# A chunked scan and two gated feed-forward layers on one core: a fourth raw-weight buffer and new queue orders

## The chip, the core and the metric

The kernel runs on one core of one Trainium2 chip. A core has five engines with a queue each: PE (TensorE, matrix products), DVE (VectorE), ACT (ScalarE), POOL (GpSimd) and SP (SyncE, which here issues every DMA). Each engine works through its queue strictly in order and waits on semaphores for the others. The metric is device time in microseconds; the kernel before takes 615.63 us (median of three runs, 614.98 to 616.26).

## The reference

Three stages follow each other. The first is a linear recurrence over 4 batches, 8 heads and 768 positions, done in chunks; the other two act on each of the 3072 tokens with 256 features and a hidden width of 2048.

```python
# stage 1, per batch and head (x: 768x32, B, C: 768x16, a: 768)
log_a = np.log(np.clip(a, 1e-06, 1.0))
M = einsum(C, B) * exp(cum_i - cum_j) * causal
y = M @ x + (C @ state) * exp(cum)
state = exp(sum(la)) * state + sum_j(B_j x_j * exp(cum_end - cum_j))
# stage 2: layer 1
h = x @ w_in;  x = (h * sigmoid(h)) @ w_out
# stage 3: layer 2
h = x @ w_in2
P = a[0] + a[1]*h + a[2]*h**2 + a[3]*h**3
Q = 1 + abs(b[0])*abs(h) + abs(b[1])*h**2
out = (P / (Q + 1e-06)) @ w_out2
```

## The kernel before

**Tiles.** The 3072 tokens are 24 tiles of 128. A tile's recurrence is one *visit* on PE (`visit`, L674): four products C B (tile `att`, 32x256), four with the carried state S, eight with the masked matrix M and the token values, four for the state update. Around it DVE multiplies by the mask (`M`, L657, twice a visit), splits the result into a high and a low float32r part (`y1l`, L762), and updates the state (`um`, L745, and `S`, L749). POOL builds the mask (`Gm`, L587, four instructions a visit) and scales B and C (L604, L626). ACT makes the high part (L759) and two parity copies of C (L615).

**Layers.** The hidden width is 16 slices f of 128. Per slice and per block of tokens PE does one group of six products into `h` (in-projection: high x high, high x low, low x high, two halves each) and one of six into `acc` (out-projection). Layer 1 runs over seven blocks of 2, 2, 4, 4, 4, 4 and 4 tiles, layer 2 over six blocks of four. Blocks 0 and 1 have 256 columns, the others 512. A slice of a block goes PE `h`, then ACT and the other vector engines, then PE `acc`; blocks follow each other strictly, slice 0 to 15.

**Weights.** The weights of a slice arrive as 64-bit floats in a raw buffer (`wraw`, 512 KB, a ring of three). ACT takes the exponent and top bits (L486), DVE shifts and joins the bits (L492, L494), ACT rounds to the high part (L510), and DVE or POOL subtracts for the low part (L514). Layer 1's 16 slices are kept in 16 fixed buffers `w`. Layer 2's 16 are prepared likewise in the raw buffer, stored to `w2s` in DRAM (L526) and read back (`w<-w2s`, L536) into the same 16 buffers as the last layer-1 block lets go of them.

**Layer 2's pointwise work.** Per slice ACT does the square (L896), the absolute value (L900), the logarithm of Q (L916) and its negative exponential (L919); POOL and DVE do the polynomial (L904, L907, L910, L913), DVE the product g (L925). Then g is rounded to its high part `gh` by ACT (L801) or by POOL (L803), and POOL subtracts for the low part `gl` (L807).

**What sets the order.** Nothing is ordered by hand. The code adds operations with the engines that may run them, a cost for each, their dependencies and a sort key. `Plan.run` (L124) is a list scheduler: it repeatedly takes, among what can start soonest, the operation of the smallest key, books its cost on the engine, and so fixes every queue's order, and for operations with a choice the engine. Keys come from the table `K` (L31) and costs from the `c_*` helpers and constants in the code; the plan's model holds the time an engine needs, a port that DVE and POOL share, a factor for DVE while a mask is built (`soft`), and a slower PE where PE has had few columns. On the chip the orders stay, the times are the chip's.

Of the kernel before, what the change touches and what calls it, by code (L numbers as in the profile page):

```python
# [24 lines left out]
WC = 2 * DM  # L25
# [3 lines left out]
HALVED = 0  # L29
TAIL_FLEX = 1  # L30
K = dict(  # L31
    t0=-4.418,
    step0=0.196,
    lag1=5.7,
    fo1=-117.341,
    fo2=113.649,
    fol=49.258,
    tab=-19.458,
    lead=-17.189,
    kt=5.507,  # L40
    kq=13.452,
    kl=16.822,
    kg=-1.533,
    ks=3.696,
    warm=23,
    warm0=5.147,
    warmstep=0.414,
    late=96.836,
    tab0=255.655,
    bulk=40.355,  # L50
    d0=-10.314,
    gap0=-1.906,
    d2=0.536,
    d3=-0.323,
    early2=28.205,
    early=88.368,
    w2a=-581.064,
    w2b=-104.957,
    w1=-58.843,
    w1step=-16.262,  # L60
    w1load=15.211,
    tokload=-28.356,
    ahead=-3.939,
    eps=0.032,
    step2=9.745,
    dT=[-7.22, -13.03, -30.38, -32.69, -14.27, -104.22, 51.53, 29.37, 26.09, 41.72, 4.01, -1.19],
    dD=[-119.66, -78.65, -1.57, 14.91, -69.27, 21.05, -99.93, -46.8],
    dW=[16.35, -10.16, -80.03, 81.03, -22.98, 4.59, 58.27, 59.37, 3.02, 47.31, 26.94, 7.79, -83.78, -4.56, -23.9, -13.94],
)
SET_LN_EXP, SET_SILU = 6, 18  # L70

# [37 lines left out]
class Plan:  # L109
# [9 lines left out]
    def add(self, choices, key, deps=(), new=(), use=(), wr=(), rd=(), cols=0, after=0.0, big=True, soft=False):  # L119
        op = Op(choices, key, list(deps), list(new), list(use), wr, rd, cols, after, big, soft)  # L120
        self.ops.append(op)
        return op

    def run(self):  # L124
        free = dict.fromkeys(("PE", "ACT", "DVE", "POOL", "SP"), 0.0)
        waiting = {}
        left = {}
        for op in self.ops:
            deps = set(op.deps)
            for b in op.new:  # L130
                i = b.ring.turns.index(b)
                if i:
                    deps.update(b.ring.turns[i - 1].users[:1])
                if i >= b.ring.n:
                    deps.update(b.ring.turns[i - b.ring.n].users)
            deps.discard(op)
            op.waits = deps
            left[op] = len(deps)
            for d in deps:
                waiting.setdefault(d, []).append(op)  # L140
        ready = [op for op in self.ops if not left[op]]
        for op in ready:
            op.ready = {e: op.after for e in op.choices}
        order = []

        port = [0.0]

        def shared(op, e):
            c = op.choices[e]
            return len(c) > 2 and c[2]  # L150


        wrote, was_read = {}, {}


        ticks = {}
        wide, soft = [True], [0.0]

        def length(op, e, start):
            t = op.choices[e][0]  # L160
            if e == "DVE" and shared(op, e) and start < soft[0]:
                t *= 1.3
            if op.soft:
                soft[0] = start + t
            if e == "PE":
                if op.big != wide[0]:
                    t += 0.1
                    wide[0] = op.big
                if ticks.get(int((start + self.TICK0) / self.TICK) - 1, 0) < 3060:
                    t *= 2  # L170
                for i in range(4):
                    k = int((start + self.TICK0 + (i + 0.5) / 4 * t) / self.TICK)
                    ticks[k] = ticks.get(k, 0) + op.cols / 4
            return t

        def when(op, e):
            t = max(free[e], op.ready[e])
            for b in op.wr:
                t = max(t, was_read.get(b, 0.0))
            for b in op.rd:  # L180
                t = max(t, wrote.get(b, 0.0))
            if shared(op, e):
                t = max(t, port[0])
            return t

        while ready:
            cand = [(when(op, e), op, e) for op in ready for e in op.choices]
            first = min(c[0] for c in cand) + K["eps"]
            est, op, e = min((c for c in cand if c[0] <= first), key=lambda c: (c[1].key, c[0], c[1].choices[c[2]][0]))
            ready.remove(op)  # L190
            op.start, op.eng = est, e
            op.end = est + length(op, e, est)
            free[e] = op.end
            if shared(op, e):
                port[0] = op.end
            for b in op.wr:
                wrote[b] = op.end + self.LAT[e]
            for b in op.rd:
                was_read[b] = max(was_read.get(b, 0.0), op.end + self.LAT[e])
            order.append(op)  # L200
            for o in waiting.get(op, ()):
                left[o] -= 1
                if not left[o]:
                    o.ready = {
                        q: max(d.end + (self.LAT[d.eng] if d.eng != q or q == "SP" else self.SELF[q]) for d in o.waits)
                        for q in o.choices
                    }
                    ready.append(o)
        assert len(order) == len(self.ops), "a cycle"
        return order  # L210
# [3 lines left out]
def ssd_moe_moe_kernel(ctx: ExitStack, tc: tile.TileContext, tok, la_in, consts, w1, w2, ab, outT):  # L214
# [11 lines left out]
    ACT, DVE, POOL, PE = nc.scalar, nc.vector, nc.gpsimd, nc.tensor  # L226
    plan = Plan()
    add = plan.add
# [3 lines left out]
    def ring(tag, n, cols, dt=F32, space="SB"):  # L232
        rings[tag] = (Ring(n), n, cols, space)
# [44 lines left out]
        PE.matmul(out, lhsT, rhs, start=start, stop=stop)  # L278

    def dma(key, nbytes, fn, deps=(), new=(), use=()):  # L280
        return add({"SP": (max(0.06, nbytes / 260e3), fn)}, key, deps, new, use)


    con = fixed("con", [P, C_CUM])
# [12 lines left out]
    wide = w1.dtype == U64  # L297
    for f in range(NF):
        ring(f"w{f}", 1, 2 * WC)
    ring("wraw", 3, 2 * WC)  # L300
    if wide:
        ring("wv", 6, WC)
    ring("tok", 4, TOK + DM)
# [36 lines left out]

    cum = new("cum")
    ld_la = dma(0.0, 98e3, lambda: (load_table(SET_LN_EXP), nc.sync.dma_start(la, la_in)))
    ld_c1 = dma(0.1, 70e3, lambda: nc.sync.dma_start(con[:, 0:C_MASK], consts[:, 0:C_MASK]))

    def f_cum():
# [291 lines left out]
    def cb_part(n):  # L637
        t, T, d, ld, o_bw, o_cx, o_cw, o_gm, Gm, x, bw, cw, bt, cx, e0, Ee = at[n]
        cb = R_cb.new(lambda: att)

        def f_cb():
            for q in range(4):
                r = slice(32 * q, 32 * q + 32)
                mm(att[q][:, 0:DM], bt()[r], cx()[r], True, True)

        return cb, f_cb
# [20 lines left out]
    def cb_alone(n):  # L667
        t, T, d, o_cx = at[n][0], at[n][1], at[n][2], at[n][5]
        cb, f_cb = cb_part(n)
        o_cb = add({"PE": (0.61, f_cb)}, T + 2 * d, [o_cx], new=[cb], use=[t], wr=range(4), cols=4 * DM, big=False)  # L670
        masked(n, cb, o_cb)


    def visit(n):  # L674

        t, T, d, ld, o_bw, o_cx, o_cw, o_gm, Gm, x, bw, cw, bt, cx, e0, Ee = at[n]
# [5 lines left out]
        pv = prev.get(n - 1) if c > 0 else None  # L682
# [13 lines left out]
        def f_u():  # L696
            for q in range(4):
                r = slice(32 * q, 32 * q + 32)
                mm(psu[r], bw()[:, r], x()[:, 64 * q : 64 * q + 64], True, True)

        us = c < TPB - 1
        if us:
            ub, sn = R_psu.new(lambda: psu), new("S")
        y_deps, y_use = o_m + [o_cw] + ([pv[1]] if pv else []), ms + [t] + ([pv[0]] if pv else [])
        y_len = 0.55 + (0.25 if pv else 0)
        if n < ALONE:
            o_y = add({"PE": (y_len, f_y)}, T + 5 * d, y_deps, new=[yb], use=y_use, wr=[0, 1], cols=P, big=False)
            if us:
                o_u = add({"PE": (0.21, f_u)}, T + 4 * d, [o_bw], new=[ub], use=[t], wr=[2], big=False)
            if n + 1 < min(NTB, ALONE + 1):  # L710
                cb_alone(n + 1)
        else:
            more = n + 1 < NTB
            if more:
                cb, f_cb = cb_part(n + 1)

            def f_visit():
                if more:
                    f_cb()
                f_y()  # L720
                if us:
                    f_u()

            o_y = o_u = add(
                {"PE": (y_len + (0.15 if us else 0) + (0.61 if more else 0), f_visit)}, T + 5 * d,
                y_deps + ([o_bw] if us else []) + ([at[n + 1][5]] if more else []),
                new=[yb] + ([ub] if us else []) + ([cb] if more else []), use=y_use + ([at[n + 1][0]] if more else []),
                wr=range(4), cols=P + (4 * DM if more else 0), big=False,
            )
            if more:  # L730
                masked(n + 1, cb, o_y)
# [249 lines left out]
    t = K["t0"]  # L981
# [68 lines left out]
    for op in plan.run():  # L1050
        fn = op.choices[op.eng][1]
# [69 lines left out]
```

## Time and profile before

| | |
|---|---|
| median of three runs | 615.63 us (614.98 to 616.26) |
| profiled execution | 617.0 us, its span 615.3 us |
| mean granted clock of PE | 0.986 |
| busy: PE, DVE, ACT, POOL | 601.0, 440.5, 399.1, 366.7 us |

The span is what the rows show; the profiled execution's own time is 1.7 us longer than its span. Busy shares are means over unlike stages: the early part, in which the weights of layer 1 are prepared and the first visits run, the six blocks of layer 1 after it, and layer 2 from about 320 us.

### The profile page before, as it was taken

Reading aid. Unit: us, or ns where it says so; the run is one execution under the profiler, and the core shown is the slowest. Engines: PE = TensorE matmul, PEld = TensorE weight load, DVE = VectorE, ACT = ScalarE, POOL = GpSimd, SP = SyncE. Lnnn points to the kernel's source line nnn. Section 1 sums busy time; section 2 is a strip of 40 time slices with the busy share of each in tenths; the row PEclk is TensorE's granted clock in tenths of the full one; section 3 lists DMA queues with packets and bytes.
Section 4 is the critical chain, followed back from the end, with each engine's and each line's share of the span. In section 5 each row is a group of like instructions: output and inputs, shape, how many; then the busy total and the mean of one; then the engine's idle time right before and its main releaser. Section 6 shows DMA issues by size and latency. Waiting matters only on the chain.

```text
span 615.3 us, 9815 instructions
## 1 busy us (share of the span) xinstructions
PE 601.0 (98%) x3442; PEld 478.4 (78%) x3445; DVE 440.5 (72%) x727; ACT 399.1 (65%) x751; POOL 366.7 (60%) x478
## 2 busy tenths in 40 slices
PE   8798999999999999999999999999999999999997
PEld 4476799877777778888888887878888878878875
DVE  4899897777543412322312899998998999999995
ACT  5675686656423311312335889998988998988984
POOL 5797783423332222212200789889888888888884
PEclk8798999999999999999999999999999999999999
DMA  6765567666200000000035800000000000000000
GB/s 222 257 184 180 163 243 242 226 231 236 91 27 2 0 1 1 0 1 0 1 102 178 267 2 0 1 35 1 1 35 1 36 2 0 35 2 0 35 2 35
DMA packets 18314, 47.30 MB, mean 77 GB/s; under 512 B 2136, under 2 KB 5336, under 8 KB 18264
## 3 DMA queue, kind: packets, MB, share of 16 engines
q1 hardware_dynamic: 18264, 46.67, 22.5%
q8 instruction: 27, 0.44, 0.3%
q14 instruction: 23, 0.19, 0.1%
HBM read 34.99 MB, written 11.67 MB: 76 GB/s over the span
## 4 chain that ended last, share of the span: by engine, by line
PE 87%; DVE 6%; POOL 2%; ACT 2%; issue 1%; DMA 1%; SPq 0%; DVEq 0%; ACTq 0%; POOLq 0%
PE acc L278 41%; PE h L278 34%; PE b L278 7%; PE att L278 5%; POOL Gm L587 1%; DVE wv L494 1%; POOL gl L807 1%; DMA tok<-in_tok_dram 1%; DVE M L657 1%; DVE gl L807 1%; DVE tok L913 1%; DVE g L925 1%; DVE h L910 0%; ACT wv L486 0%; ACT tok L615 0%
## 5 line engine op out<-in xcount | busy, mean ns | idle before, releaser
L278 PE MATMUL h<-y1h,w 128*128 128x512 f32 (+1 forms) x700 | 222.8, 376 | 1.1 <-POOL w L514 0.9
L278 PE MATMUL acc<-gh,w 128*128 128x512 f32 (+1 forms) x832 | 215.3, 380 | 1.0 <-ACT gh L801 1.0
L278 PEld LDWEIGHTS acc<-gh,w 128*128 128x128 f32 x832 | 149.8, 189 | 33.5 <-ACT gh L801 1.4
L807 DVE TENSOR_TENSOR gl<-T,gh 128x512 fp32r<-128x512 f32 (+1 forms) x101 | 68.0, 674 | 120.0 <-POOL gh L803 88.6
L278 PEld LDWEIGHTS h<-y1h,w 128*128 128x128 f32 x700 | 129.6, 190 | 29.5 <-DVE tok L913 2.1
L839 ACT ACTIVATE T<-h 128x512 f32<-128x512 f32 (+1 forms) x112 | 59.7, 534 | 118.5 <-PE h L278 111.4
L278 PE MATMUL h<-y1l,w 128*128 128x512 f32 (+1 forms) x350 | 130.4, 373 | 0.0
L807 POOL TENSOR_TENSOR gl<-g,gh 128x512 fp32r<-128x512 f32 x95 | 122.9, 1299 | 11.5 <-ACT gh L801 7.5
L803 POOL TENSOR_SCALAR gh<-T 128x512 fp32r<-128x512 f32 (+1 forms) x59 | 35.9, 608 | 154.7 <-ACT T L839 123.1
L278 PE MATMUL acc<-gl,w 128*128 128x512 f32 (+1 forms) x416 | 124.3, 379 | 0.2 <-DVE gl L807 0.2
L278 PEld LDWEIGHTS acc<-gl,w 128*128 128x128 f32 x416 | 76.3, 189 | 16.3 <-DVE gl L807 0.4
L904 POOL TENSOR_SCALAR tok<-T,abt 128x512 f32<-128x512 f32 x96 | 74.5, 776 | 11.6 <-ACT T L896 9.8
L278 PEld LDWEIGHTS h<-y1l,w 128*128 128x128 f32 x350 | 66.4, 190 | 11.4
L925 DVE SCALAR_TENSOR_TENSOR g<-tok,abt,b 128x512 f32<-128x512 f32 x96 | 71.3, 744 | 4.6 <-POOL gl L807 1.6
L907 DVE SCALAR_TENSOR_TENSOR b<-T,absb,b 128x512 f32<-128x512 f32 x96 | 71.8, 749 | 1.4 <-ACT b L900 1.4
L916 ACT ACTIVATE b<-b,lnb 128x512 f32<-128x512 f32 x96 | 63.6, 664 | 7.1 <-DVE b L907 6.3
L587 POOL TENSOR_SCALAR_AFFINE_SELECT Gm<-eG 128x256 f32<-128x256 f32 x96 | 55.4, 611 | 20.7 <-DVE M L657 14.0
L919 ACT ACTIVATE b<-b 128x512 f32<-128x512 f32 x96 | 56.3, 588 | 1.6
L910 DVE TENSOR_TENSOR h<-tok,h 128x512 f32<-128x512 f32 x63 | 43.4, 689 | 5.3 <-ACT b L900 5.3
L913 DVE SCALAR_TENSOR_TENSOR tok<-T,abt,h 128x512 f32<-128x512 f32 x63 | 46.7, 741 | 0.0
L278 PE MATMUL b<-y1h,w 128*128 128x512 f32 x132 | 46.4, 392 | 0.0
L803 POOL TENSOR_SCALAR gh<-g 128x512 fp32r<-128x512 f32 x59 | 36.8, 624 | 14.3 <-PE acc L278 12.5
(68 smaller groups left out, 649.6 us busy)
## 6 DMA issues: line engine op xcount, KB each, us to landing
wraw<-in_w_dram SPq DMA_DIRECT2D x32, 512.0 KB, 4.4
w2s<-wraw SPq DMA_DIRECT2D x16, 512.0 KB, 2.9
w<-w2s SPq DMA_DIRECT2D x16, 512.0 KB, 4.7
tok<-in_tok_dram SPq DMA_DIRECT2D x24, 320.0 KB, 3.0
out_dram<-Gm SPq DMA_DIRECT2D x12, 256.0 KB, 2.0
Ee<-dre SPq DMA_DIRECT2D x21, 66.5 KB
cum<-in_consts_dram SPq DMA_DIRECT2D x1, 320.0 KB
dre<-Ee SPq DMA_DIRECT2D x2, 66.5 KB
```

The costliest lines, as they stand in the source:

```text
L278: PE.matmul(out, lhsT, rhs, start=start, stop=stop)
L587: POOL.affine_select(g4[:, :, p * SUB : (p + 1) * SUB], eG[:, p, n * H : (n + 1) * H].unsqueeze(2).broadcast_to([P, H, SUB]), pattern=[[0, ...
L803: eng.tensor_scalar(gh.t[:, 0:W], g.t[:, 0:W], 1.0, 0.0, op0=ALU.mult, op1=ALU.add)
L807: eng.tensor_tensor(gl.t[:, 0:W], g.t[:, 0:W], gh.t[:, 0:W], op=ALU.subtract)
L839: ACT.activation(T.t[:, 0:W], h.t[:, 0:W], AF.Silu)
L904: POOL.tensor_scalar(t1.t[:, 0:W], s.t[:, 0:W], abt[:, 3:4], abt[:, 1:2], op0=ALU.mult, op1=ALU.add)
L907: DVE.scalar_tensor_tensor(c.t[:, 0:W], s.t[:, 0:W], absb[:, 1:2], c.t[:, 0:W], op0=ALU.mult, op1=ALU.add)
L910: DVE.tensor_tensor(h.t[:, 0:W], t1.t[:, 0:W], h.t[:, 0:W], op=ALU.mult)
L913: DVE.scalar_tensor_tensor(t1.t[:, 0:W], s.t[:, 0:W], abt[:, 2:3], h.t[:, 0:W], op0=ALU.mult, op1=ALU.add)
L916: ACT.activation(c.t[:, 0:W], c.t[:, 0:W], AF.Ln, bias=lnb)
L919: ACT.activation(c.t[:, 0:W], c.t[:, 0:W], AF.Exp, scale=-1.0)
L925: DVE.scalar_tensor_tensor(g.t[:, 0:W], t1.t[:, 0:W], abt[:, 0:1], c.t[:, 0:W], op0=ALU.add, op1=ALU.mult)
```

## The change

The ring of raw weights has four buffers instead of three. Four cost constants of the plan change: the rate of a DMA (260 to 380 KB per us), the length of a visit on PE, and the factor on DVE beside a mask (1.3 to 1.4). Nearly all numbers of the table `K` are new. No operation is added or removed; the numbers of PE, DVE and SP instructions are the same.

```diff
-    t0=-4.418,
+    t0=29.745,
...
-    w1load=15.211,
+    w1load=-66.668,
...
         def length(op, e, start):
             t = op.choices[e][0]
             if e == "DVE" and shared(op, e) and start < soft[0]:
-                t *= 1.3
+                t *= 1.4
...
     def dma(key, nbytes, fn, deps=(), new=(), use=()):
-        return add({"SP": (max(0.06, nbytes / 260e3), fn)}, key, deps, new, use)
+        return add({"SP": (max(0.06, nbytes / 380e3), fn)}, key, deps, new, use)
...
-    ring("wraw", 3, 2 * WC)
+    ring("wraw", 4, 2 * WC)
...
-        y_len = 0.55 + (0.25 if pv else 0)
+        y_len = 0.55 + (0.33 if pv else 0)
...
-                {"PE": (y_len + (0.15 if us else 0) + (0.61 if more else 0), f_visit)}, T + 5 * d,
+                {"PE": (y_len + (0.21 if us else 0) + (0.64 if more else 0), f_visit)}, T + 5 * d,
```

The orders that come out differ on every engine. The first place is DVE at the end of layer 1's weight preparation, in the kernel before. `w_67` is the buffer of slice 15, `wv` a weight under way, `gl` the low part of a layer-1 slice, `M`, `um`, `S` and `y1l` belong to visits.

```order
L657 TENSOR_TENSOR M_1063<-att_80,Gm_927 128x512
L762 TENSOR_TENSOR y1l<-att_80,y1h 128x2x128
L657 TENSOR_TENSOR M_1074<-att_81,Gm_927 128x512
L492 TENSOR_SCALAR wv_1078<-wv_1078 128x512
L749 SCALAR_TENSOR_TENSOR S_1096<-S_1007,Ee_772,um_1058 128x64
L494 SCALAR_TENSOR_TENSOR wv_1078<-wraw_998,wv_1078 128x512
L807 TENSOR_TENSOR gl_1123<-T_1115,gh_1117 128x256
L514 TENSOR_TENSOR w_67_1121<-wv_1078,w_67_1121 128x512
L762 TENSOR_TENSOR y1l<-att_80,y1h 128x2x128
```

And the same place in the changed kernel (the last row of both is the one behind slice 15's low part):

```order
L807 TENSOR_TENSOR gl_920<-T_855,gh_858 128x256
L494 SCALAR_TENSOR_TENSOR wv_884<-wraw_811,wv_884 128x512
L807 TENSOR_TENSOR gl_951<-T_897,gh_901 128x256
L492 TENSOR_SCALAR wv_947<-wv_947 128x512
L807 TENSOR_TENSOR gl_962<-T_942,gh_945 128x256
L494 SCALAR_TENSOR_TENSOR wv_947<-wraw_882,wv_947 128x512
L514 TENSOR_TENSOR w_64_953<-wv_884,w_64_953 128x512
L610 TENSOR_TENSOR tok_868<-tok_868,Ee_918 128x128
L514 TENSOR_TENSOR w_67_975<-wv_947,w_67_975 128x512
L745 TENSOR_TENSOR um_996<-att_81,con 128x64
```

Ahead of slice 15's low part DVE had the masks of twelve visits, and has those of nine: 18 instead of 24 multiplications `M`, 8 instead of 11 `y1l`, 5 instead of 8 each of `um` and `S`, 11 instead of 12 `gl`, but 10 instead of 9 low parts of weights and 9 instead of 8 scalings of C (L610). On PE twelve visits stood ahead of slice 15's first `h` group, and nine do now; the tenth now stands at the end of block 1, and the eleventh to the eighteenth between the groups of block 2, with two or three `h` or `acc` groups of 512 columns between two visits (eight of them, mostly, before). POOL builds 41 instead of 53 mask instructions in that stretch.

The second place is ACT in the middle of layer 2: `h` and `b` are banks of `h` or of the running Q, `T` the square. Before:

```order
L896 ACTIVATE T_4788<-h_3707 128x512
L916 ACTIVATE b_3494<-b_3494,lnb 128x512
L919 ACTIVATE b_3494<-b_3494 128x512
L900 ACTIVATE b_3492<-h_3707,abt 128x512
L916 ACTIVATE b_3493<-b_3493,lnb 128x512
L896 ACTIVATE T_4818<-b_3491 128x512
L919 ACTIVATE b_3493<-b_3493 128x512
L801 ACTIVATE gh_4831<-g_4793 128x512
L900 ACTIVATE b_3494<-b_3491,abt 128x512
```

After:

```order
L896 ACTIVATE T_4873<-h_3598 128x512
L900 ACTIVATE b_3471<-h_3598,abt 128x512
L801 ACTIVATE gh_4885<-g_4871 128x512
L919 ACTIVATE b_3472<-b_3472 128x512
L916 ACTIVATE b_3471<-b_3471,lnb 128x512
L896 ACTIVATE T_4901<-h_3670 128x512
L900 ACTIVATE b_3470<-h_3670,abt 128x512
L801 ACTIVATE gh_4913<-g_4899 128x512
L919 ACTIVATE b_3471<-b_3471 128x512
L916 ACTIVATE b_3470<-b_3470,lnb 128x512
```

Before, high parts `gh` stand on ACT for 37 of layer 2's 96 slice and block pairs and on POOL for 59; now for 80 and 16. One turn of ACT is now square, absolute value, `gh`, exponential, logarithm, in this order.

Of the other places two are told in words. Between the last layer-1 use of slice 0's buffer on PE and layer 2's first `h` group on it stood six groups of 512 columns (three `acc`, three `h`), and stand three (two `acc`, one `h`); the read of its layer-2 weights is issued behind that last use. And of layer 2, PE's order after the start is one `h` and one `acc` in turn, with `acc` six slices behind `h`, where it was eight.

## Rows read from the trace of the kernel before

**Rows 1.** Windows: stretch, length, busy (instructions) of PE, PEld, DVE, ACT, POOL; clock

```profile
0.00:8.59 8.59, 6.67 (x33) 3.69 (x34) 1.20 (x5) 3.91 (x10) 1.38 (x9) 1.00 0.74 225
8.59:27.90 19.31, 14.57 (x154) 8.86 (x155) 17.20 (x33) 12.41 (x29) 16.39 (x30) 0.73 0.69 237
27.90:54.00 26.10, 24.29 (x277) 18.52 (x278) 24.77 (x46) 19.81 (x51) 22.27 (x36) 1.00 0.64 205
54.00:66.00 12.00, 10.52 (x107) 8.16 (x108) 9.34 (x19) 4.96 (x13) 7.87 (x15) 0.72 0.44 142
66.00:76.70 10.70, 10.12 (x122) 7.97 (x120) 9.77 (x20) 7.30 (x19) 8.77 (x13) 1.00 0.54 176
76.70:108.30 31.60, 31.56 (x355) 28.81 (x356) 27.31 (x56) 22.28 (x56) 19.21 (x35) 1.00 0.71 242
400.00:600.00 200.00, 199.94 (x862) 160.58 (x861) 190.03 (x292) 180.70 (x318) 174.20 (x190) 1.00 0.04 14
```

**Rows 2.** Groups of DVE instructions, whole span, shapes apart

```profile
L657 DVE TENSOR_TENSOR M<-att,Gm 128x512 f32<-128x512 f32 x48 | 32.3, 682 | 1.4 <-ACT y1h L759 0.8 <-POOL tok L604 0.3
...
L807 DVE TENSOR_TENSOR gl<-T,gh 128x256 fp32r<-128x256 f32 x26 | 14.4, 556 | 2.2 <-ACT gh L801 1.1 <-issue 0.6 <-POOL gh L803 0.4
...
L762 DVE TENSOR_TENSOR y1l<-att,y1h 128x256 fp32r<-128x256 f32 x24 | 10.0, 416 | 6.3 <-ACT y1h L759 6.0 <-PE att L278 0.2
...
L610 DVE TENSOR_TENSOR tok<-tok,Ee 128x128 f32<-128x128 f32 x16 | 6.7, 421 | 1.5 <-DMA tok<-in_tok_dram 1.4
...
L749 DVE SCALAR_TENSOR_TENSOR S<-S,Ee,um 128x64 f32<-128x64 f32 x16 | 5.6, 353 | 0.1
...
L745 DVE TENSOR_TENSOR um<-att,con 128x64 f32<-128x64 f32 x16 | 3.5, 217 | 3.3 <-PE att L278 3.0 <-ACT Ee L419 0.3
```

**Rows 3.** Timeline of DVE from 65 to 77 us

```profile
66.02 0.69 DVE L494 SCALAR_TENSOR_TENSOR wv<-wraw,wv 128x512 uint32<-128x512 uint32 x1
...
69.97 0.91 DVE L494 SCALAR_TENSOR_TENSOR wv<-wraw,wv 128x512 uint32<-128x512 uint32 x1
...
75.98 0.70 DVE L514 TENSOR_TENSOR w<-wv,w 128x512 fp32r<-128x512 f32 x1
```

**Rows 4.** Timeline of POOL, the mask instructions beside it

```profile
68.70 2.49 POOL L587 TENSOR_SCALAR_AFFINE_SELECT Gm<-eG 128x256 f32<-128x256 f32 x4
```

**Rows 5.** Chain that ended last, 97 to 103 us: start, length, what

```profile
98.20 1.42 PE acc L278 x12
99.62 1.71 PE att L278 x40
101.33 0.92 PE acc L278 x6
```

**Rows 6.** Waits, 8.59 to 76.7 us: total, times, longest

```profile
PE att L278 <- DVE M L657: 4.4, 4, 2.5
...
DVE w L514 <- ACT w L510: 2.4, 3, 1.8
...
ACT wv L486 <- DMA wraw<-in_w_dram: 0.8, 2, 0.5
```

**Rows 7.** DMA issues of the page: KB each, median us to landing

```profile
w<-w2s SPq DMA_DIRECT2D x16, 512.0 KB, 4.7
```

**Rows 8.** All transfers that touch the tensor w2s

```profile
DMA to landing us min/median/max: 2.9/3.7/5.1
```

**Rows 9.** Timeline of ACT in layer 2

```profile
467.99 0.60 ACT L896 ACTIVATE T<-h 128x512 f32<-128x512 f32 x1 [0.66 <-PE h L278]
468.49 0.66 ACT L900 ACTIVATE b<-h,abt 128x512 f32<-128x512 f32 x1
469.06 0.63 ACT L801 ACTIVATE gh<-g 128x512 fp32r<-128x512 f32 x1
469.58 0.66 ACT L916 ACTIVATE b<-b,lnb 128x512 f32<-128x512 f32 x1
470.18 0.66 ACT L900 ACTIVATE b<-h,abt 128x512 f32<-128x512 f32 x1
```

More of the change, by code (lines that the diff above doesn't have):

```diff
@@ L31 @@
 K = dict(
-    t0=-4.418,
[L33 to L44, printed above, removed]
+    t0=29.745,
+    step0=29.431,
+    lag1=-8.285,
+    fo1=-11203.308,
+    fo2=3770.147,
+    fol=4732.874,
+    tab=348.639,
+    lead=521.411,
+    kt=-2007.807,
+    kq=185.136,
+    kl=885.523,
+    kg=-42.381,
+    ks=-46.369,
     warm=23,
@@ L47 @@
     warmstep=0.414,
[L48 to L60, printed above, removed]
-    w1load=15.211,
[L62 to L68, printed above, removed]
+    late=129.205,
+    tab0=262642.37,
+    bulk=-71.654,
+    d0=1.385,
+    gap0=-2.671,
+    d2=-175.049,
+    d3=1.526,
+    early2=13.234,
+    early=102.236,
+    w2a=-179.125,
+    w2b=922.116,
+    w1=27.105,
+    w1step=-47.852,
+    w1load=-66.668,
+    tokload=-25.637,
+    ahead=-12.045,
+    eps=0.045,
+    step2=553.546,
+    dT=[28.53, 94.46, -154.25, -63.99, -191.58, -193.3, 23.14, -88.64, 60.15, 62.96, 55.27, -29.82],
+    dD=[-161.27, -199.56, 54.31, 2.45, -51.6, -13.37, -139.38, -52.27],
+    dW=[17.78, -91.6, -65.39, 20.75, -87.36, -2.84, 152.31, 99.55, -14.36, 54.11, 87.31, 7.07, -116.76, -71.36, 56.44, -4.52],
 )
```

## The prediction

> **What bounds the kernel now.** I read the windows of all engines first [rows 1]. From 76.7 us on PE has no idle time worth a name (31.56 of 31.60 us busy, then 199.94 of 200.00 in layer 2), at full clock. What is left there is work, and the change leaves the work as it is. All that can be won or lost by an order lies ahead of 76.7 us, or in making PE wait where it doesn't now. Ahead of 76.7 us PE is idle for 1.92 + 4.74 + 1.81 + 1.48 + 0.58 = 10.5 us, and twice its clock is low: 0.73 and 0.72 granted are 54% and 56% of the stretch at 1.2 instead of 2.4 GHz.
>
> PE is not what holds this stretch back. The end of it, 76.7 us, is where DVE finishes the low part of slice 15, layer 1's last weight [rows 3]; blocks run strictly one behind the other, so block 1 and all that follows stand behind slice 15. DVE is busy for 1.20 + 17.20 + 24.77 + 9.34 + 9.77 = 62.3 of the 76.7 us. Of the 14.4 idle, 7.4 lie before 8.59 us, when the first weight arrives; the other 2.11 + 1.33 + 2.66 + 0.93 = 7.0 are all that a better order can take from DVE. PE's waits for the mask products and DVE's for ACT's high part [rows 6] are two sides of this: DVE's queue is full, and each detour over ACT or PE costs it a little.
>
> So the end is: the time at which DVE has slice 15, and after it PE's remaining work, provided that nothing stalls PE again.
>
> **The change, term by term.** The sum is made against the profiled execution, 617.0 us with a span of 615.3; that lies 1.4 us above the median of the runs, 615.63, to which I carry the result.
>
> *Less on DVE ahead of slice 15.* Three visits fewer stand there. That is 6 mask products of 0.682, 3 splits of 0.416, 3 updates of 0.217 and 0.353, and one low part of 0.556, less one more weight's low part (0.70) and one scaling (0.421): 4.09 + 1.25 + 0.65 + 1.06 + 0.56 - 0.70 - 0.42 = 6.5 us [rows 2, 3]. Neighbours overlap: all of DVE's instructions to slice 15 at their groups' means are 66.4 us, and 62.3 were busy, a factor 0.94. Hence -6.1 us.
>
> *The same work later on PE.* The three visits don't vanish. A visit is 1.71 us, and the group behind it 0.92 instead of 0.71 (half of 1.42), so 1.92 each; one out-projection group of 0.71 moves over too [rows 5]. 3 x 1.92 + 0.71 = +6.5 us. The two terms cancel but for 0.4: leaving visits for later is no gain by itself.
>
> *Less of POOL beside DVE.* The same instruction took DVE 0.69 us at 66.02 and 0.91 at 69.97, when POOL was building a mask [rows 3, 4]. If four kinds of DVE instructions per weight, 16 each, lengthen so by 0.2 two times in three, contention costs some 8.5 us. Three masks fewer are 3 x 2.49 = 7.5 of POOL's 1.38 + 16.39 + 22.27 + 7.87 + 8.77 = 56.7 us, 13%. I take -1.1 us; the ends are 0 and twice that. The Trainium skill, "SBUF — State Buffer", section "SBUF: two separate sides", says that DVE and GpSimd hold their common port as an exclusive lock and that the loser fully blocks; by that a hit would cost up to the rest of a POOL instruction, at most 2.49 / 4 = 0.62 here, and the term up to three times as much, -3. The rows show 0.22 and decide.
>
> *DVE's stalls.* The fourth raw buffer can save at most what ACT waited for raw weights in this stretch, 0.8 us in two waits [rows 6]. The rest of the 7.0 comes from the places of the other instructions: DVE waited 2.4 us for ACT's high part, 1.8 of them once, in the stretch from 54 to 66 us where PE is at half clock. In the new order the first mask is followed by the scalings of B, not by two more masks, and the factors' round trip through DRAM starts sooner, so that the fourth weight's load leaves some 2 us earlier; two weights' bits stand closer together. Against that, PE has three visits' work less to do in the same stretch, so it has more gaps and may lose its clock as often. Ends: all 7.0 gone, or 3 us more than now (the stretch from 54 to 66 us once again, 2.66). No row shows the new order's stalls; I take -2.0, nearer to no change than to all gone.
>
> *The read of layer 2's weights.* The first `h` group of layer 2 now stands three groups behind the last use of its buffer. A pair of groups in layer 2 is 12 products, 199.94 / 862 x 12 = 2.78 us, so three groups are 4.2 us [rows 1]. The 512 KB take 4.7 us (median) to land [rows 7], and between 2.9 and 5.1 for all transfers of that tensor [rows 8]. PE then waits between 0 and 1.1 us; I take 0.5. Behind PE's waiting group stand three groups of layer 1, and nothing waits for those. The skill's "DMA: Bandwidth & Descriptors", section "Anatomy of one DMA — SWDGE (gpsimd) path", fits 2.0 us and 436 KB per us, an estimate of 3.2 us for 512 KB and no wait, which would make the sum 0.5 lower; the fit is for another issuing engine, and the 4.7 stands.
>
> *Visits packed into block 2.* Eight visits now stand with two or three groups of 4.2 us at most between them. A visit's mask products wait for the products of the visit before it and need 2 x 0.682 on DVE, so they fit; per visit DVE has 2.35 us there, one weight of layer 2 and two low parts, against some 6 us of PE. In the stretch to 76.7 us PE waited 4.4 us for mask products over twelve visits [rows 6]; eight at that price are 2.9. Ends 0 and 2.9; I take 0.8, since DVE in this stretch has PE's full 6 us per visit.
>
> *ACT in layer 2.* 43 high parts move from POOL to ACT. A turn is now square, absolute value, high part, exponential, logarithm. By starts, square to the next 0.50, absolute value 0.57, high part 0.52, logarithm 0.60 [rows 9]; with 0.50 for the exponential, which has the square's size, 2.69 us against PE's 2.78. From the other side: ACT is busy 180.70 us for 862 / 12 = 71.8 turns with 25 high parts, 2.52 a turn; 43 / 96 more of 0.63 are 0.28, so 2.80. The first is made of starts in a packed queue, which is what the new one is; I take it, and 0 for the term. Were it the second, ACT would set the pace. What is queued behind a late ACT is everything, since `h` banks come free through it.
>
> The sum: -6.1 + 6.5 - 1.1 - 2.0 + 0.5 + 0.8 + 0 = -1.4. That is 615.6 for the profiled execution and 614.2 for the median.
>
> **Rivals.** *Nearly all stalls go* (-6 instead of -2): 610.2. For it: the stall around 54 to 66 us is a chain of one late visit, a low clock and a low part behind it, and a plan with truer costs may not form it; against it: every detour over ACT and PE is still there.
>
> *Only the swap* (the stalls stay as they are, +2.0): 616.2, no difference that can be told. For it: the two large terms cancel, and DVE is at 24.77 of 26.10 us already in the longest stretch. Against it: less of POOL.
>
> *ACT becomes the bound of layer 2*, the rival on the other side. Its place is the turn of five; it decides as soon as a turn takes more than PE's 2.78 us. If the logarithm must wait for DVE's operand (ACT is idle 19.3 us of 200, 0.27 a turn, today), a quarter of that on top of 2.80 makes 2.87, and 0.09 x some 55 turns costs 4.8: 619.0. For it: 2.80 from one side. Against it: the starts, and 0.09 us of room.
>
> *Visits in block 2 stop PE and cost it its clock*: 2.9 us instead of 0.8, and behind such idle time a stretch as that from 54 to 66 us, whose 56% at half clock cost 0.56 x 10.52 / 2 = 2.9: 614.2 + 2.1 + 2.9 = 619.2. For it: two such stretches are in the trace, each with PE idle. Against it: PE's groups of 512 columns lie between, and in the rows behind 76.7 us PE is never below full clock [rows 1]. [...]
>
> **How the numbers follow.** The forecast has 0.42 (its own range 612.0 to 615.6, from the stalls' middle part), nearly all stalls gone 0.20, only the swap 0.14, ACT 0.13, packed visits 0.11. A measurement of this kernel tells 0.2%, 1.2 us, from no change: below 614.4 is faster, above 616.9 slower. Of the forecast's 0.42 I count 0.27 as faster and 0.15 as the same. Faster: 0.27 + 0.20 = 0.47. Same: 0.15 + 0.12 = 0.27, with most of the swap. Slower: 0.13 + 0.11 + 0.02 = 0.26. The range of 8 in 10 reaches from 609.5, nearly all stalls gone, to 618.5, most of the two slower cases.
>
> **What would show it.** Right: slice 15's low part on DVE near 67 to 68 us, with some 5 us of DVE idle behind 8.6 us; PE's work behind it longer by 6.5; a wait of PE below 1 us at layer 2's first `h` group; PE above 199.5 of 200 us in layer 2. Wrong: slice 15 later than 70.5 us (no gain then by any path), gaps of PE before mask products between 95 and 150 us, an ACT without idle time in layer 2 while PE has some, or a low clock behind slice 15.

## The result: slower by 0.6%

The changed kernel takes 621.40 us (median of 4 runs, 619.76 to 622.50) against 615.94 us for the kernel before on the same chip (4 runs); the ratio is 1.0057, with a 95% interval of 1.0031 to 1.0083. I had forecast 614.2 us and a range to 618.5, so both the sign and the range were wrong. The profiled execution took 622.5 us with a span of 620.5.

### The profile page after: what moved, and what is told of

Same layout as the page of the kernel before. It is cut to its first block, busy times and chain, and to the rows that moved or that the text cites. A ratio compares the mean times of both kernels' runs of the same rounds, so it can differ in the third digit from the quotient of the medians.

```text
span 620.5 us, 9831 instructions
## 1 busy us (share of the span) xinstructions
PE 601.7 (97%) x3445; PEld 477.1 (77%) x3445; DVE 439.9 (71%) x727; ACT 411.6 (66%) x790; POOL 346.7 (56%) x439
## 4 chain that ended last, share of the span: by engine, by line
PE 80%; DMA 11%; DVE 4%; ACT 3%; issue 1%; SPq 0%; POOL 0%; DVEq 0%; ACTq 0%
PE acc L278 39%; PE h L278 30%; PE b L278 7%; DMA w2s<-wraw 7%; DMA wraw<-in_w_dram 4%; PE att L278 4%; ACT wv L486 1%; DVE wv L494 1%; DMA tok<-in_tok_dram 1%; DVE M L657 1%; DVE wv L492 1%; DVE gl L807 0%; DVE w L514 0%; ACT tok L615 0%; ACT T L839 0%
## 5 line engine op out<-in xcount | busy, mean ns | idle before, releaser
L803 POOL TENSOR_SCALAR gh<-T 128x512 fp32r<-128x512 f32 (+1 forms) x63 | 38.1, 605 | 151.8 <-ACT T L839 120.2
L587 POOL TENSOR_SCALAR_AFFINE_SELECT Gm<-eG 128x256 f32<-128x256 f32 x96 | 54.1, 596 | 23.7 <-DVE M L657 14.6
L919 ACT ACTIVATE b<-b 128x512 f32<-128x512 f32 x96 | 58.1, 605 | 0.5
L801 ACT ACTIVATE gh<-g 128x512 fp32r<-128x512 f32 x80 | 51.4, 642 | 2.8 <-DVE g L925 2.5
```

The costliest lines, as they stand in the source:

```text
L587: POOL.affine_select(g4[:, :, p * SUB : (p + 1) * SUB], eG[:, p, n * H : (n + 1) * H].unsqueeze(2).broadcast_to([P, H, SUB]), pattern=[[0, ...
L801: ACT.activation(gh.t[:, 0:W], g.t[:, 0:W], AF.Copy)
L919: ACT.activation(c.t[:, 0:W], c.t[:, 0:W], AF.Exp, scale=-1.0)
```

## The profile after

First the windows of all engines, cut as in [rows 1], with one more stretch from 108.3 to 160 us; the row behind them is that stretch in the kernel before.

```profile
8.59:27.90 19.31, 18.90 (x167) 10.65 (x164) 16.03 (x32) 10.95 (x27) 16.16 (x28) 0.67 0.68 225
27.90:54.00 26.10, 22.17 (x249) 17.55 (x248) 25.22 (x50) 20.40 (x50) 20.42 (x31) 1.00 0.68 215
54.00:66.00 12.00, 11.17 (x137) 9.27 (x137) 11.61 (x23) 8.69 (x22) 8.77 (x13) 1.00 0.63 210
66.00:76.70 10.70, 10.48 (x87) 10.27 (x87) 10.29 (x20) 8.24 (x21) 6.00 (x11) 1.00 0.48 193
76.70:108.30 31.60, 30.69 (x278) 25.60 (x276) 21.55 (x47) 20.10 (x46) 13.64 (x23) 1.00 0.68 207
108.30:160.00 51.70, 45.48 (x384) 31.61 (x384) 34.40 (x66) 26.41 (x54) 30.64 (x50) 0.97 0.68 222
400.00:600.00 200.00, 200.00 (x869) 162.81 (x868) 195.34 (x296) 195.57 (x359) 157.06 (x157) 1.00 0.04 14
```

```profile
108.30:160.00 51.70, 51.70 (x307) 40.20 (x306) 38.01 (x67) 31.14 (x59) 17.52 (x27) 1.00 0.66 226
```

Ahead of 76.7 us the new order is the better one: from 8.59 us on PE is idle for 5.4 us (8.6 before), and the stretch from 54 to 66 us, at a granted clock of 0.72 before, is at full clock. The loss stands where PE had none: 0.91 us idle up to 108.3 and 6.22 up to 160. The largest piece is 4.45 us, with a low clock right behind it (the columns are the same):

```profile
120.00:130.00 10.00, 5.55 (x56) 3.67 (x55) 4.56 (x11) 4.62 (x11) 3.97 (x8) 1.00 0.83 272
130.00:140.00 10.00, 10.00 (x80) 6.64 (x80) 8.07 (x14) 5.57 (x11) 7.45 (x11) 0.83 0.64 178
```

What PE waits for there is spread over many lines (the waits of PE from 100 to 160 us: releaser, us in total, times, longest):

```profile
PE h L278 <- ACT T L839: 2.9, 1, 2.9
PE acc L278 <- POOL gl L807: 1.6, 1, 1.6
PE att L278 <- ACT wraw L510: 1.0, 1, 1.0
PE acc L278 <- ACT gh L801: 0.9, 1, 0.9
PE att L278 <- DVE y1l L762: 0.7, 1, 0.7
```

None of these is a mask product, which is what I had watched for. The chain of waits (start, length, what) shows one thing behind the longest of them. It runs in a loop through DRAM from 77 us on:

```profile
93.50 4.65 DMA wraw<-in_w_dram
...
98.18 0.69 ACT wv L486
...
98.89 0.44 DVE wv L492
...
99.35 0.50 DVE wv L494
...
99.85 5.59 DMA w2s<-wraw
...
105.93 5.02 DMA w2s<-wraw
...
111.35 6.88 DMA w2s<-wraw
...
118.68 5.43 DMA w2s<-wraw
...
124.12 4.57 DMA wraw<-in_w_dram
...
128.72 0.66 ACT wv L486
...
129.38 0.50 ACT T L839
```

A weight of layer 2 is read raw (L469), converted on ACT, DVE and POOL, and stored split (L526). The chain goes from a store to the next load, because that load reuses the store's buffer. SP's timeline, after and then before, shows where each stands:

```profile
99.47 0.33 SPq L469 DMA_DIRECT2D wraw<-in_w_dram  x1
99.85 0.43 SPq L526 DMA_DIRECT2D w2s<-wraw  x1
100.39 0.36 SPq L558 DMA_DIRECT2D tok<-in_tok_dram  x1
100.80 1.10 SPq L576 DMA_DIRECT2D Ee<-dre  x1
105.50 0.33 SPq L469 DMA_DIRECT2D wraw<-in_w_dram  x1
105.93 0.38 SPq L526 DMA_DIRECT2D w2s<-wraw  x1
```

```profile
96.80 0.33 SPq L526 DMA_DIRECT2D w2s<-wraw  x1
97.22 0.38 SPq L469 DMA_DIRECT2D wraw<-in_w_dram  x1
101.42 0.33 SPq L558 DMA_DIRECT2D tok<-in_tok_dram  x1
102.32 1.16 SPq L526 DMA_DIRECT2D w2s<-wraw  x1
103.54 0.42 SPq L469 DMA_DIRECT2D wraw<-in_w_dram  x1
```

Before, a load was issued behind the *next* store (mostly 0.4 us) and never waited for its own. Now it is the first raw load behind the very store that it waits for, with the next store 0.4 us behind it. From 101.90, the end of the issue at 100.80, to 105.50 us SP stands. In the waits of SP's queue from 60 to 160 us, after and then before:

```profile
SPq L469 <- DMA w2s<-wraw: 40.9, 12, 5.4
```

```profile
SPq L526 <- DVE wraw L514: 32.6, 11, 4.3
```

Before, stores waited for their data, and PE was busy for 51.70 of 51.70 us beside it; now loads wait for stores to land, and the conversion waits behind them (waits from 90 to 160 us; before, ACT waited 0.4 us once in the same stretch):

```profile
DVE wv L492 <- ACT wv L486: 14.4, 8, 3.8
ACT wv L486 <- DMA wraw<-in_w_dram: 14.4, 9, 2.5
```

Layer 1's `T`, `gh` and `gl` and the visits' `y1h` stand in the queues of ACT and DVE behind the waiting conversion: ACT turns to the raw weight at 128.72 us and only then, at 129.38, makes the `T` for which PE waits 2.9 us. POOL, besides, waits 8.6 us for decay factors and token data (0.2 before), which SP also loads. That the wait at SP's head sets PE's stalls is the theory tested below, called **A**. The rivals: **B**, eight visits packed into block 2 stop PE by their own chain; **C**, the transfers merely slow one another.

## The experiments

Each ratio is to the kernel before, run beside it on the same chip, and stands with its 95% interval.

**Six raw buffers, orders kept.** The tiles are taken from a pool of six; the plan still counts four.

```
-        rings[tag] = (Ring(n), n, cols, space)
+        rings[tag] = (Ring(n), 6 if tag == "wraw" else n, cols, space)
```

> The changed kernel with six raw-weight buffers in SBUF while the plan still counts four, so the order on every engine stays as it is and only the waits for a buffer go. Theory A (SP's queue stands at the head in a load that waits for the store of its own buffer to land, 40.9 us of such waits between 60 and 160 us, and ACT's conversion and with it the visits of block 2 wait behind): the SP waits on w2s<-wraw fall below 5 us, PE's idle time between 108.3 and 160 us falls from 6.2 to under 2.5 us, and the time is 614 to 617 us, level with the kernel before. Rival B (visits packed into block 2 stop PE by their own chain on DVE and ACT, whatever the raw weights do): the SP waits go, PE's idle time there stays at 5 to 6 us, and the time stays at 620 to 622. Rival C (load and store slow one another in the DMA engines): loads and stores take longer still, over 5 us each, ACT waits for raw weights as before, 620 to 623.

Measured: 612.23 us, 0.9917 (0.9896 to 0.9939): from 1.0057 that is 1.4%, 8.6 us, and more than A asked. SP has no wait for a store any more, ACT's for raw weights are 3.5 us, PE's idle time in the stretch 1.8 us:

```profile
108.30:160.00 51.70, 49.88 (x418) 36.54 (x420) 38.19 (x69) 28.02 (x57) 33.89 (x53) 1.00 0.59 189
```

With the orders of all engines the same, the waits for a raw buffer alone made the changed kernel slower. B and C fall as the main cause; part of the wait is still that a store lands later beside a load (last section).

The two kernels can be held side by side, instruction by instruction. The same instruction of ACT starts 0.9 us later in the changed kernel at 80 us (80.91 against 79.99), 9.75 later at 158 us (158.42 against 148.67) and 9.75 later at 588 us (588.19 against 578.44). So all of the difference but the first 0.9 us arises between 80 and 158 us.

**The load behind the next store**, with four buffers; only SP's queue is altered.

```
-    for op in plan.run():
+    order = plan.run()
+    for ld in loads:
+        i = order.index(ld)
+        j = next((k for k in range(i + 1, len(order)) if order[k] in stores), None)
+        if j is not None and i and any(o in stores for o in order[:i]):
+            order.insert(j, order.pop(i))
+    for op in order:
```

> The changed kernel with four buffers and the planned order, in which only SP's queue is altered: each load of a raw weight of layer 2 is issued behind the next store, not directly behind the store of the buffer that it reuses, as it stood in the kernel before. A: by the time that the load is at the head its store has landed, so the SP waits on w2s<-wraw fall from 40.9 to under 12 us and the time to 615 to 618 us. B: no change, 620 to 622. C: a load still runs beside a store, so their times and PE's idle time stay, 620 to 622.

Measured: 618.69 us, 1.0021 (1.0004 to 1.0037), some 2 us off the changed kernel (the two intervals just overlap) and just past the edge of A's forecast. SP's waits for stores fall to 6.0 us, but the load now stands behind a store that itself waits for its data, and ACT still waits 8.6 us for raw weights; PE is idle 4.2 us in the stretch. One place in the queue is traded for another.

**The opposite edit in the kernel before**: each load directly behind the store of its own buffer.

```
+    for ld in loads:
+        mine = [o for o in stores if o in ld.waits]
+        if mine:
+            order.remove(ld)
+            order.insert(order.index(mine[-1]) + 1, ld)
```

> The kernel before with only SP's queue altered the other way: each load of a raw weight of layer 2 directly behind the store of the buffer that it reuses, as in the changed kernel. If the wait at SP's head costs by itself: 20 to 40 us of SP waits on w2s<-wraw appear, ACT waits for raw weights, PE idles 2 to 5 us between 76 and 160 us, 618 to 621 us. If it costs only where visits are packed into the same stretch: the SP waits appear, PE stays busy, 615 to 617 us. B alone: 615 to 616.5.

Measured: 629.59 us, 1.0189 (1.0163 to 1.0215): slower by 12 us, beyond both cases that I had given. The waits of SP's queue and the window (the edit puts this line 1 lower, L470):

```profile
SPq L470 <- DMA w2s<-wraw: 56.8, 13, 5.1
```

```profile
108.30:160.00 51.70, 46.77 (x286) 35.80 (x286) 34.61 (x62) 25.98 (x50) 17.27 (x28) 0.94 0.62 200
```

The wait costs by itself, with visits as thinly spread as before; that it costs only where visits are packed is refuted. Of the 12.6 us that the profiled span is longer, 2.6 are there before the first moved load: slice 15's low part ends at 79.25 us against 76.68, in a stretch whose granted clock is 0.87 where it was 1.00 (27.9 to 54 us). Some 10 us are left for the edit. But the way is another than in the changed kernel. ACT hardly waits for raw weights; what comes late are the visits' token data and decay factors, whose loads stand behind the raw load in SP's queue (waits from 76 to 200 us, and 8.4 us more for decay factors; all such waits before: 0.2):

```profile
POOL tok L608 <- DMA tok<-in_tok_dram: 6.6, 1, 6.6
DVE tok L614 <- DMA tok<-in_tok_dram: 4.9, 1, 4.9
ACT wv L489 <- DMA wraw<-in_w_dram: 0.4, 1, 0.4
```

The wait at SP's head is the common part; which engine it reaches depends on what stands behind it.

**The fourth buffer alone**, in the kernel before with its orders (a pool of four, the plan counts three).

```
-        rings[tag] = (Ring(n), n, cols, space)
+        rings[tag] = (Ring(n), 4 if tag == "wraw" else n, cols, space)
```

> The kernel before with a fourth raw-weight buffer in SBUF and every order as it was: the buffer alone. The prediction gave at most 0.8 us for it (ACT's waits for raw weights between 8.59 and 76.7 us): 615.1 to 616.2 us. A says nothing more, since in that order no load waits for a store at SP's head; B the same.

Measured: 617.63 us, 1.0007 (0.9990 to 1.0024). No gain that can be told: the prediction's "at most 0.8" stands.

**The plan told the landing time.** Only the cost of one kind of operation in the plan is altered, and all queues are planned anew with the changed kernel's keys and four buffers.

```
+            st = dma(key + 0.4, P * WC * 8, f_out, [o], new=[dr], use=[part])
+            st.lat = 4.2
...
-   d.end + (self.LAT[d.eng] if ...
+   d.end + (d.lat or self.LAT[d.eng] if ...
```

> The changed kernel with four buffers in which only the plan's own figure is mended: a store of a layer-2 weight is said to land 4.2 us behind the end of its issue (5.6 us in all, as the trace of the changed kernel shows) in place of 2.0, and all queues are planned anew from there with the same keys. A: the plan now sets token and decay loads ahead of the raw loads, SP's waits on w2s<-wraw fall to 10 to 25 us, but the raw weights still come one per landing, so ACT waits in part as before: 614 to 619 us. If the plan's figure were not the fault: 620 to 623 us.

Measured: 611.49 us, 0.9905 (0.9877 to 0.9933), better than forecast and level with six buffers. SP's waits for stores do not vanish (25.3 us, the upper end of the forecast), but ACT waits for raw weights only 5.0 us, in seven small pieces, and PE is idle 0.9 us. The weights are spread over more time: the last store is issued at 165.4 us, at 152.7 in the changed kernel.

```profile
SPq L469 <- DMA w2s<-wraw: 25.3, 7, 5.5
```

```profile
108.30:160.00 51.70, 50.77 (x426) 37.94 (x423) 39.81 (x74) 32.22 (x61) 26.01 (x42) 1.00 0.66 209
```

So mending one figure is enough: 512 KB at the new rate of 380 KB per us and 2.0 of latency let the plan believe that a store lands 3.4 us after its issue. Since every engine's queue comes out in another order, the run doesn't show by which of the new places the time is won.

**Six buffers, loads one store earlier.**

```
+    for i, ld in enumerate(loads[4:]):
+        order.remove(ld)
+        order.insert(order.index(stores[i - 1]) + 1 if i else order.index(loads[3]) + 1, ld)
```

> The changed kernel with six raw-weight buffers and SP's queue altered in one way: each raw load of layer 2 stands one store earlier than planned (behind the store before the one whose buffer the plan meant), so it waits at most for a store two places ahead. A: neither SP nor ACT waits for the raw round any more (ACT's waits for raw weights between 76 and 160 us from 14.4 to under 1.5 us), PE's idle time between 108.3 and 160 us falls under 0.7 us, 608.5 to 611.5 us. B: idle time of 1.5 us and more stays in that stretch with no raw weight in its chain, 611.5 to 614. C (load and store slow one another): stores and loads run together more than in any run so far, visits' token loads come late, 612 to 616.

Measured: 612.01 us, 0.9914 (0.9888 to 0.9941). ACT's wait for raw weights is down to 0.2 us and PE's idle time in the stretch to 0.6, as A said, so the packed visits' own price (B) in idle time of PE is at most that:

```profile
108.30:160.00 51.70, 51.11 (x425) 37.23 (x424) 39.90 (x71) 28.95 (x59) 33.91 (x55) 1.00 0.52 177
```

SP still waits 13.3 us for stores, against A's forecast of none, without ACT or PE waiting for it. The time did not follow: it is level with the plain six buffers, and the 1.2 us less of idle time appear as 0.6 us of span. The difference is within the intervals.

**Six raw buffers, and five each for token data and decay factors**, orders kept.

```
-        rings[tag] = (Ring(n), n, cols, space)
+        rings[tag] = (Ring(n), {'wraw': 6, 'tok': 5, 'Ee': 5}.get(tag, n), cols, space)
```

> The changed kernel with six raw-weight buffers (as in the first run) and, besides, five buffers for a token slice's data and five for its decay factors in place of four each; all orders as planned. In the run with six raw buffers SP still stood 48.0 us in loads of token data that wait for a visit to be done with the buffer, with the raw loads behind them; the one stall of PE left between 100 and 160 us (1.6 us at 122) began with ACT waiting 1.42 us for a raw weight. A (what reaches ACT late through SP's queue sets PE's stalls): SP's waits for att fall to 10 to 25 us, that stall goes, 609 to 612 us. B (packed visits have a price of their own): 1.5 us and more of idle PE stay between 108.3 and 160 us, 611.5 to 614.

Measured: 604.35 us, 0.9779 (0.9749 to 0.9808): 8 us under six raw buffers alone, where A gave 0 to 3. PE has no idle time from 108.3 to 160 us, but that explains 1.8 us. Much of the rest is in layer 2, where PE is not idle in either run from 400 to 590 us. The groups of PE's products there (count, busy, mean ns; neighbouring products overlap), in the run with six raw buffers and then here:

```profile
L278 PE MATMUL acc<-gh,w 128*128 128x512 f32 x276 | 75.1, 393 | 0.0
...
L278 PE MATMUL acc<-gl,w 128*128 128x512 f32 x137 | 43.2, 395 | 0.0
```

```profile
L278 PE MATMUL acc<-gh,w 128*128 128x512 f32 x280 | 75.0, 389 | 0.0
...
L278 PE MATMUL acc<-gl,w 128*128 128x512 f32 x140 | 43.1, 389 | 0.0
```

The same product takes 389 ns and not 393 to 395, and 840 of all products fit into 190 us and not 826, one in 226 ns and not 230. With the tiles of two rings in another pool, `gh` and `gl` had moved in SBUF (to 132352 bytes per partition from 148864). That they set the pace by their place is theory **D**, tested below against rival **T**, the fifth buffers themselves.

**Both at once**: the loop over `loads` of the run before last, and the line of the last one.

> Both at once: six raw buffers, raw loads one store earlier, five buffers each for token data and decay factors. A: nothing is left for it over the earlier loads, 608 to 611.5 us, within 1 us of the run with the earlier loads. C: more transfers at once, 612 to 616.

Measured: 602.66 us, 0.9766 (0.9738 to 0.9794), the fastest kernel of the study, 2.3% under the kernel before and 2.9% under the changed one (0.9766 / 1.0057 = 0.971). It lies under the forecast; theory D, tested next, gives the larger part of that.

**`gh` and `gl` 128 bytes further**, by a longer tile ahead of them, in four kernels: the changed one, the one before, the one with six raw buffers, and the one whose plan was told the landing time. All orders stay as they were.

```
-    ring("Ee", 4, P + R5)
+    ring("Ee", 4, 144)
...
-            Ee.t = Ee.make()
+            Ee.t = Ee.make()[:, 0 : P + R5]
```

> The changed kernel with its four raw buffers and every order as planned; each of the four decay-factor tiles is 44 bytes longer per partition, so the tiles gh and gl behind them start 128 bytes further in SBUF (165376 in place of 165248 per partition). The run with five token and decay buffers had come out 8 us under the run without them, with PE's matmuls on gh and gl at 389 ns each in place of 394 to 396, and there gh started at 132352. Theory D (the place of gh and gl in SBUF, 0 or 128 bytes past a multiple of 256, sets the pace of the matmuls that stream them): matmuls acc<-gh at 389 to 390 ns, 840 of the matmuls of layer 2 in 190 us in place of 826, the time 7 to 10 us under the changed kernel: 611 to 614.5. Rival T (the fifth token and decay buffers themselves gave the 8 us, through SP's queue and layer 2's t1 tiles, which share them): no change, 620 to 622, matmuls at 394.

Measured: 615.71 us, 0.9968 (0.9947 to 0.9988).

```profile
L278 PE MATMUL acc<-gh,w 128*128 128x512 f32 x280 | 75.0, 389 | 0.3 <-DVE Gm L964 0.3
...
L278 PE MATMUL acc<-gl,w 128*128 128x512 f32 x140 | 43.1, 389 | 0.0
```

> The kernel before with the same longer decay-factor tiles, every order as it was: gh starts at 148992 in place of 148864. D: 606 to 609 us, ratio 0.984 to 0.989, matmuls at 389 to 390 ns; T: 615 to 617 us.

Measured: 611.76 us, 0.9920 (0.9889 to 0.9951).

> The changed kernel with six raw buffers (the first run, 0.9917 of the kernel before) and gh moved by the same 128 bytes; four token and decay buffers. D: 603 to 606 us, as the run with five token buffers (604.4), whose fifth buffers then brought little; T: 611 to 613.

Measured: 606.79 us, 0.9833 (0.9808 to 0.9858).

> The run whose plan was told that a store lands 5.6 us after its issue (four raw buffers, 0.9905 of the kernel before), with gh moved by the same 128 bytes. D: 602 to 605 us; T: 610.5 to 612.5.

Measured: 605.77 us, 0.9813 (0.9789 to 0.9837).

D holds in all four for the pace, and T in none: the products on `gh` and `gl` take 389 to 390 ns wherever these start at a multiple of 256 bytes per partition. Other tiles behind the longer one moved too; but with five token buffers the tile `g` starts 160 bytes past such a multiple, as the program places it, and the products take 389 ns all the same. The times lie 0.8 to 2.8 us above D's forecasts. Ratio by ratio the shift gives 0.9911, 0.9920, 0.9915 and 0.9907, so 5 to 6 us and not the 7 to 10 that I had read off one difference; the other 3 us (0.9779 against 0.9833) do belong to the fifth buffers and to PE's idle time that went with them. The shift is no part of the change: in both kernels, and with six raw buffers, `gh` starts 128 bytes past such a multiple, so the experiments with four token buffers are not touched by it.

## Why the prediction was wrong, point by point

- *Less on DVE, less of POOL beside it, and DVE's stalls* (-6.1, -1.1 and -2.0): right in their sum, and a little short; only the sum and DVE's idle time can be read. Slice 15's low part ends on DVE at 65.17 + 0.68 = 65.85 us against 75.98 + 0.70 before [rows 3], 10.8 us earlier where I had 9.2; DVE is idle for 4.6 us from 8.59 to 66 where I gave "some 5". In the runs that have the same order up to there it ends at 64.9 (six buffers) and 65.4 us (the load behind the next store), so a single trace tells it to 1 us.

```profile
65.17 0.68 DVE L514 TENSOR_TENSOR w<-wv,w 128x512 fp32r<-128x512 f32 x1
```

- *The same work later on PE* (+6.5): right as far as it can be read. With six buffers slice 15's low part ends at 64.21 + 0.68 = 64.89 us, 11.8 earlier than before, and the terms give 615.3 - 11.8 + 6.5 - 2.2 (layer 2, below) + 1.8 (idle) = 609.6; the profiled span is 610.8.
- *The read of layer 2's weights* (+0.5): 0. No wait of PE at that place.
- *ACT in layer 2* (0, and the rival of an ACT bound): the rival fell. ACT is busy 195.57 of 200 us [rows 1: 180.70], yet PE has no idle time and does 869 products where it did 862. Over the 1152 products of layer 2 that is 1152 x (200 / 862 - 200 / 869) = 2.2 us gained. ACT's turn, by the same sums as in the prediction, is 195.57 / (869 / 12) = 2.70 us: the price by starts, 2.69, was right and the one by busy time, 2.80, was not. Why the new order is faster there was not tried.
- **The step that failed is "Visits packed into block 2"**, +0.8 with ends of 0 and 2.9. I priced that stretch by the waits for mask products [rows 6] and by DVE's room, and had the ends from there too. PE lost 0.91 + 6.22 us there, and at a clock of 0.83 from 130 to 140 us, a third of it at the lower level, 1.7 more. What I left out was in the diff: the DMA rate of the plan and the fourth buffer set when a raw load is *allowed* in SP's queue, and I looked at SP only for the reads of layer 2's split weights. I never asked what stands at the head of SP's queue between 76 and 160 us. The windows [rows 1] had shown PE without idle time from 76.7 to 108.3 us and in layer 2, and the row shown above is as full: a new wait there could only lose. What the runs show in its place is the wait of raw loads at SP's head for stores to land, 40.9 us in twelve; without it the changed kernel is 8.6 us faster.
- The rival *Packed visits stop PE and its clock* (619.2, chance 0.11) had the right place, the right sign and the low clock behind the idle time, but not the cause: with the loads out of the way, the same eight visits leave PE idle for 0.6 us or less.
- The terms as measured give 615.3 - 10.8 + 6.5 - 2.2 + 7.1 + 1.7 = 617.6 us of span against 620.5 seen; 2.9 us stay open. The low clock from 8.59 to 27.9 us, 0.67 against 0.73 [rows 1], can't fill them, for it lies ahead of slice 15 and is in the 10.8; it is 1.00 there in the kernel with the load behind the next store, so it varies from run to run. Between the changed kernel and six buffers, 8.8 us arise from 80 to 158 us: 5.3 are idle time of PE (7.1 against 1.8), 1.7 the clock, and 1.8 stay open too.

## What to carry to other kernels

In a queue that is served in order, ask of every entry what it waits for once it is at the head, and what stands behind it; a load into a ring of buffers that is queued directly behind the store it waits for puts that store's whole landing time into the loop. A plan's figure for a transfer has to be the time to landing beside the transfers that the plan itself will put next to it: a bare rate and latency (3.4 us) led it into an order in which a store takes 5 to 7. And when a stretch has no idle time, price the change there by every queue that feeds it.

## What the hardware showed beside that

- A 512 KB store that goes out first, with the next load behind it, mostly by 0.4 us, lands in 2.9 us in the kernel before (its stores: 2.9 at least, at the median and at most). Behind a load, issued 0.4 us ahead of it in the changed kernel, it takes about 5 us and more: 5.02 to 6.88 in the chain above, 4.95 to 5.30 in the chain of the kernel before with its loads moved, where the load is 0.4 to 1.9 us ahead. The Trainium skill, "DMA: Bandwidth & Descriptors", section "Anatomy of one DMA — SWDGE (gpsimd) path", says that a wait for a semaphore is made by the issuing engine before it hands the transfer over, and fits 2.0 us plus the bytes by 436 KB per us for transfers that GpSimd issues, an estimate of 3.2 us. The 40.9 us in which SP stood agree with the first; the second is near the lone store and far from the other.
- The place in SBUF of the operand whose columns stream through PE (`gh`, `gl`) sets the pace of the products of 512 columns: 393 to 395 ns at 128 bytes past a multiple of 256, 389 to 390 at the multiple, and 5 to 6 us of 620 in all. Only starts at 0, 256 and 384 bytes past a multiple of 512 were seen, so which multiple counts stays open, as does the reason.
- With that pace the kernel before does 826 products in 190 us and the changed one 840: something beside PE's pace holds layer 2 in the order of before. What it is was not tried.
